# Moving two dummy matmuls from behind a weight piece to in front of it, and one cast from GpSimd to VectorE, in the start of an attention plus MoE kernel

## The chip, the cores and the metric

One core of a Trainium2 chip. The metric is the device time of one execution in microseconds (us), the median of several.

## The reference

```python
def _attn_ref(x, state):                # x [8, 8, 512, 64], state [8, 8, 32, 64]
    scores = scale * np.matmul(x, state.transpose(0, 1, 3, 2))
    a = softmax(scores)                 # (written out in the original)
    xread = np.matmul(a, state)
    scores2 = scale * np.matmul(state, x.transpose(0, 1, 3, 2))
    a2 = softmax(scores2)
    sread = np.matmul(a2, x)
    return np.concatenate([xread, sread], axis=2)

def _moe_ref(x, w_in, w_out):           # 4352 tokens, 512 -> 2048 -> 512
    h = x @ w_in
    g = h * (1.0 / (1.0 + np.exp(-h)))
    return g @ w_out
```

The kernel never forms `xread`. For each batch it multiplies the states by `w_in` (this product is called W1) and applies the normalized scores `a` to W1, which gives the hidden layer at once. So before the first output matmul, batch 0 needs its scores, their transposes, and at least the first columns of W1.

## The kernel before

The loads at the start, in the order of the GpSimd queue. In the trace before the pieces land in this order too, the first at about 8.2 us and the columns 512 to 1023 at 15.5:

```python
    load_w_in(0, 128)        # first W1 piece
    load_w_in(128, 384)      # second W1 piece
    load_w_out(0, 2)         # output weights, blocks 0 and 1
    load_w_out(2, 2)
    nc.gpsimd.dma_start(st1_n..., state[1]...)
    load_w_in(512)           # columns 512 to 1023
    load_w_out(4, 4)
    # ... cut; the rest is issued later
```

The second half of batch 0's input is cast in four quarters, by ScalarE (two), GpSimd and VectorE:

```python
    cast_x(0, nc.scalar, 2, 2, 4, 4)
    cast_x(0, nc.gpsimd, 0, 1, 4, 4)
    pe_transpose_x(0, 0, 2, new_o, (nc.vector, nc.vector))
    cast_x(0, nc.vector, 1, 1, 4, 4)
```

`keep_busy(n, ...)` issues n matmuls on zeros, 128x512 each, whose results nobody reads: dummies, meant to keep TensorE warm while it waits (in the trace before, the first seven, from cold, come 0.43 us apart, later ones 0.216). The stage of the change:

```python
    norm(0, 0)                                    # product on GpSimd
    scores(0, 1, 2); exps(0, 1)                   # (two lines)
    norm(0, 1, ((nc.vector, 0, 4),), 2)           # product on VectorE
    w1_cols(0, [(0, 128)], (nc.scalar, nc.scalar))
    # ... cut: more loads issued
    keep_busy(3, psH, "h1")
    pss0 = w1_mms(0, [(128, 384)])                # the second W1 piece
    keep_busy(2, psH, "h1")
    for c in (0, 2):
        # ... cut: four transposes of the GpSimd half, copies
        at_mms(ps_a, 0, 0, c, 2)
    for c in (0, 2):
        # ... cut: four transposes of the VectorE half, copies
        at_mms(ps_a, 0, 1, c, 2)
    w1_out(0, [(128, 128)], both, pss0)
    upto(1)                                       # first hidden block
    # ... cut
    for ft in range(12):                          # batch 0's output matmuls
        # at ft == 2: w1_mms(0, [(512, 512)]), the W1 matmuls of columns 512 to 1023
```

The softmax here doesn't subtract the row's maximum and nothing guards it: scores larger than these inputs give would overflow.

## Time and profile before

| | before |
|---|---|
| median of 3 runs | 213.05 us (212.82 to 213.13) |
| span of the trace | 211.5 us |
| TensorE busy | 203.7 us, 96% |
| second W1 piece starts | 10.29 us, its weights just landed |
| transposes of the normalized scores start | 11.02 us |
| W1 matmuls of columns 512 to 1023 start | 15.59 us, their weights just landed |

The view of transfers lists an issue with its size and the time from issue to landing. Here are the second W1 piece (384 KB, issued at about 2.4 us) and the columns 512 to 1023 (512 KB, issued at 5.13 us):

```profile
w_in_sb<-in_moe_w_in_dram POOLq DMA_DIRECT2D x1, 384.0 KB, 7.8
w_in_sb<-in_moe_w_in_dram POOLq DMA_DIRECT2D x1, 512.0 KB, 10.4
```

They land at about 10.2 and 15.5 us, exactly where TensorE takes them up.

### The profile page before, as it was taken

The numbers are of one execution on the slowest core, as the hardware profiler recorded it, in microseconds if no ns is written. First come the engines' busy times: TensorE is split into PE (matmuls) and PEld (weight loads), VectorE is DVE, ScalarE is ACT, GpSimd is POOL, SyncE is SP. The second block draws the span as 40 slices with busy tenths as digits, with TensorE's granted clock in tenths as the row PEclk, the third lists the DMA queues.
The fourth block names the chain that finished last, engine by engine and source line by source line (L and its number), as shares of the span: only waits on it lengthen the run. The fifth ranks groups of instructions, "written<-read, shape, count | busy, mean of one in ns | idle before, by whom it ended". The sixth has DMA issues, their size and how long they took to land.

```text
span 211.5 us, 3841 instructions
## 1 busy us (share of the span) xinstructions
PE 203.7 (96%) x1550; PEld 96.8 (46%) x1575; DVE 74.1 (35%) x146; ACT 139.3 (66%) x244; POOL 40.1 (19%) x62
## 2 busy tenths in 40 slices
PE   7799999999999999999999999999999999999993
PEld 2444454444444444444444444444444444466653
DVE  3842257657841236113410653043412306100011
ACT  3866677899577867697569855996775166644410
POOL 8672215503320042012201202000200000000000
PEclk9999999999999999999999999999999999999999
DMA  6999999995549756555935429114221111011112
GB/s 196 193 203 207 287 258 340 226 272 179 103 104 239 205 130 138 122 176 102 233 80 183 104 64 207 50 53 99 80 69 37 63 64 53 0 50 50 53 50 99
DMA packets 42929, 28.65 MB, mean 135 GB/s; under 512 B 28064, under 2 KB 37792, under 8 KB 42912
## 3 DMA queue, kind: packets, MB, share of 16 engines
q1 hardware_dynamic: 36720, 20.65, 37.4%
q0 software_dynamic: 5904, 7.64, 17.4%
q8 instruction: 12, 0.20, 0.4%
q10 hardware_dynamic: 288, 0.13, 0.2%
q14 instruction: 5, 0.04, 0.1%
HBM read 17.43 MB, written 8.91 MB: 125 GB/s over the span
## 4 chain that ended last, share of the span: by engine, by line
PE 90%; DMA 5%; POOL 2%; issue 1%; DVE 0%; POOLq 0%
PE o L566 50%; PE h L525 25%; DMA w_in_sb<-in_moe_w_in_dram 5%; PE ps_w L469 4%; PE h L546 3%; PE o_a L566 3%; PE o_part L588 2%; PE ps_sr L416 1%; PE ps_scT L332 1%; POOL w_in_sb L150 1%; POOL w_out_sb L153 1%; PE ps_sc L306 0%; PE ps_xt L253 0%; DVE W L159 0%; POOL st_n L191 0%
## 5 line engine op out<-in xcount | busy, mean ns | idle before, releaser
L566 PE MATMUL o<-w_out_sb,g 128*128 128x512 bf16 x480 | 129.5, 379 | 1.3 <-issue 0.5
L557 ACT ACTIVATE g<-h 128x512 bf16<-128x512 f32 (+1 forms) x143 | 81.3, 573 | 34.1 <-PE h L525 19.9
L566 PEld LDWEIGHTS <-g 128*128 128x128 bf16 x528 | 50.3, 98 | 59.1 <-issue 3.8
L525 PE MATMUL h<-aT,W 128*128 128x512 bf16 x247 | 73.1, 379 | 0.1
L159 DVE COPY o_sb<-o 128x512 f32<-128x512 f32 x15 | 10.4, 691 | 89.1 <-PE o L566 86.2
L525 PEld LDWEIGHTS <-W 128*128 128x128 bf16 x254 | 24.5, 98 | 30.3 <-issue 0.7
L159 DVE CAST W<-ps_w 128x512 bf16<-128x512 f32 (+2 forms) x36 | 22.2, 658 | 23.2 <-PE ps_w L469 23.2
L157 ACT ACTIVATE W<-ps_w 128x512 bf16<-128x512 f32 (+1 forms) x32 | 16.2, 562 | 11.1 <-PE ps_w L469 11.1
L159 POOL CAST x_nat<-x_f 128x512 bf16<-128x512 f32 x24 | 14.7, 655 | 35.7 <-DMA x_f<-in_x_dram 35.7
L157 ACT ACTIVATE o_sb<-o 128x512 f32<-128x512 f32 x16 | 9.5, 597 | 14.4 <-PE o L566 11.9
L362 POOL TENSOR_TENSOR an<-e,rcn 128x512 bf16<-128x512 bf16 x5 | 7.6, 1517 | 48.0 <-DVE rcn L360 48.0
L469 PE MATMUL ps_w<-w_in_sb,stT 64*32 64x512 bf16 (+2 forms) x264 | 10.3, 373 | 0.6 <-DMA w_in_sb<-in_moe_w_in_dram 0.6
L566 PE MATMUL o_a<-w_out_sb,g 128*128 128x512 bf16 x31 | 9.8, 379 | 0.2
L546 PE MATMUL h<-xmT,w_in_sb 128*128 128x256 bf16 x64 | 9.6, 273 | 0.1
L546 PEld LDWEIGHTS <-w_in_sb 128*128 128x128 bf16 x64 | 6.3, 98 | 3.9
L359 DVE TENSOR_REDUCE rs<-e 128x32 f32<-128x1024 bf16 x5 | 6.1, 1213 | 3.1 <-DMA e<-eT 3.1
L165 PE MATMUL ps_busy<-busy 128*128 128x512 bf16 x15 | 5.9, 497 | 1.2 <-DVE warm L172 1.2
L346 ACT ACTIVATE eT<-ps_scT 128x512 bf16<-128x512 f32 x10 | 5.4, 597 | 1.6 <-PE ps_scT L332 1.6
L786 ACT ACT_TABLE_LOAD x5 | 6.4, 1283 | 0.1
L469 PEld LDWEIGHTS <-stT 64*32 64x32 bf16 x264 | 3.2, 90 | 6.0 <-issue 4.1
L382 POOL TENSOR_TENSOR an<-exp_nat,rc 128x512 bf16<-128x512 bf16 x3 | 3.1, 1048 | 14.8 <-DVE rc L380 14.8
L768 ACT ACT_TABLE_LOAD x4 | 5.1, 1283 | 0.1
(76 smaller groups left out, 99.7 us busy)
## 6 DMA issues: line engine op xcount, KB each, us to landing
out_dram<-o_sb SPq DMA_DIRECT2D x33, 256.0 KB, 2.5
x_f<-in_x_dram SPq DMA_DIRECT2D x4, 1024.0 KB, 6.1
x_f<-in_x_dram POOLq DMA_DIRECT2D x2, 1024.0 KB, 11.9
w_in_sb<-in_moe_w_in_dram POOLq DMA_DIRECT2D x3, 512.0 KB, 10.5
x_f<-in_x_dram SPq DMA_DIRECT2D x2, 512.0 KB, 4.7
w_out_sb<-in_moe_w_out_dram POOLq DMA_DIRECT2D x4, 256.0 KB, 12.0
w_out_sb<-in_moe_w_out_dram POOLq DMA_DIRECT2D x2, 512.0 KB, 12.2
x_f<-in_x_dram POOLq DMA_DIRECT2D x2, 512.0 KB, 15.2
```

Of the source, the lines that this page charges most:

```text
L157: nc.scalar.activation(dst, src, func=COPY, bias=0.0)
L159: eng.tensor_copy(dst, src)
L165: nc.tensor.matmul(ps[:], busy[:, 0:128], busy[:], start=True, stop=True, skip_group_check=True)
L346: nc.scalar.activation(t[:, hg], scT_ps[hg][:], func=EXP, bias=0.0, scale=SCALE)
L359: nc.vector.tensor_reduce(rs[:], e2[b][:], axis=AX, op=ADD)
L362: eng.tensor_tensor(a[:, hg], e2[b][:, hg], rc[:, hg].to_broadcast([128, 4, 4, NS]), op=MULT)
L469: nc.tensor.matmul(pss[f, hg][ds(32 * s, 32), 0:n], stT[ds(r, 64), b, h // 2, s % 2, :], w_in_sb[ds(r, 64), h // 2, ds(f, n)], start=True, ...
L525: nc.tensor.matmul(h_ps[k][:], W1[b][:, hg, ds(128 * ft, 128)], aT[b][:, hg, :, :], start=(hg == 0), stop=(hg == 1), skip_group_check=True,)
L546: nc.tensor.matmul(ps[:, 0:256], w_in_sb[:, kt, ds(128 * ft, 128)], xmT[:, :, kt].rearrange("p t n b -> p t (n b)"), start=(kt == 0), stop ...
L557: nc.scalar.activation(g[:, 0:n], ps[:, 0:n], func=SILU, bias=0.0)
L566: nc.tensor.matmul(outs[tt][:], gt[b * NFT + ft][:, ds(128 * tt, 128)], w_out_sb[:, ft, :], start=(ft == 0), stop=(ft == NFT - 1), skip_gr ...
L786: nc.scalar.activation(warm[:], busy[:, 0:1], func=SILU, bias=0.0)
```

## The change

Its intent: GpSimd and VectorE should not cast side by side, and the dummies should fill the wait in front of the second W1 piece instead of standing between it and the transposes.

```diff
     cast_x(0, nc.scalar, 2, 2, 4, 4)
-    cast_x(0, nc.gpsimd, 0, 1, 4, 4)
     pe_transpose_x(0, 0, 2, new_o, (nc.vector, nc.vector))
-    cast_x(0, nc.vector, 1, 1, 4, 4)
+    cast_x(0, nc.vector, 0, 2, 4, 4)
 ...
-    keep_busy(3, psH, "h1")
+    keep_busy(5, psH, "h1")
     banks[:] = ["a2", "a3"]
     turn[0] = 0
     pss0 = w1_mms(0, [(128, 384)])
-    keep_busy(2, psH, "h1")
```

## The prediction

> **What bounds the kernel now.** I read the views in this order: the page's busy shares, the chain that ended last in order of time, the timelines of the first 16 us by engine, the waits, and the landing times of the weights.
>
> The busy shares say who owns the whole span:
>
> ```profile
> PE 203.7 (96%) x1550; PEld 96.8 (46%) x1575; DVE 74.1 (35%) x146; ACT 139.3 (66%) x244; POOL 40.1 (19%) x62
> ```
>
> TensorE is busy for 203.7 of 211.5 us, so only 7.8 us are idle. The 40-slice row shows TensorE's digits below 9 only in the first two slices (7 and 7, to 10.6 us) and the last. The change lies between 6.6 and 11.7 us, in the start where something is to be had. But what matters is what holds TensorE after it, and there the chain speaks:
>
> ```profile
> 5.13 10.42 DMA w_in_sb<-in_moe_w_in_dram
> 15.55 0.04 issue
> 15.59 0.62 PE ps_w L469 x16
> 16.22 0.32 PE o L566
> ```
>
> Read from the bottom: the matmuls that build W1 from the columns 512 to 1023 of the input weight start at 15.59, 0.04 us after the transfer of these columns landed at 15.55. That transfer was issued at 5.13 and took 10.42 us. Before it the chain lists only GpSimd issuing transfers, back to the first microsecond. Nothing that TensorE, VectorE or GpSimd compute between 5.13 and 15.55 is on it. From 15.59 on the chain is TensorE almost without a break. So the end is set by "weights landed at 15.55" plus TensorE's work from there.
>
> Is TensorE waiting there, or does it only happen to arrive? Its timeline and that of its weight loads:
>
> ```profile
> 14.74 0.81 PE L566 MATMUL o_a<-w_out_sb,g 128*128 128x512 bf16 x3
> 15.47 0.26 PEld L469 LDWEIGHTS <-stT 64*32 64x32 bf16 x16 [0.42 <-issue]
> 15.59 0.62 PE L469 MATMUL ps_w<-w_in_sb,stT 64*32 64x512 bf16 x16
> ```
>
> At the next two such places (21.43 and 26.62) weight load and first matmul start within 0.01 us of one another. Here the matmul starts 0.12 us after its weight load. I read these 0.12 us as a short wait for the landing: TensorE would have been ready at about 15.47. It has no slack against this transfer, it already waits a little.
>
> The stage of the change itself:
>
> ```profile
> 6.61 0.47 POOL L159 CAST x_rows<-x_f 128x256 bf16<-128x256 f32 x1
> 6.65 0.58 DVE L159 CAST x_rows<-x_f 128x256 bf16<-128x256 f32 x1
> ...
> 7.13 0.67 PE L253 MATMUL ps_xt<-ident,x_rows 128*128 128x128 bf16 x8
> ...
> 8.89 0.82 PE L165 MATMUL ps_busy<-busy 128*128 128x512 bf16 x2
> 9.08 1.05 POOL L382 TENSOR_TENSOR an<-exp_nat,rc 128x512 bf16<-128x512 bf16 x1 [2.00 <-DVE rc L380]
> ...
> 9.98 0.70 DVE L382 TENSOR_TENSOR an<-exp_nat,rc 128x512 bf16<-128x512 bf16 x1
> ...
> 10.29 0.36 PE L469 MATMUL ps_w<-w_in_sb,stT 64*32 64x384 bf16 x8 [0.57 <-DMA w_in_sb<-in_moe_w_in_dram]
> ...
> 10.57 0.60 PE L165 MATMUL ps_busy<-busy 128*128 128x512 bf16 x2
> ...
> 11.02 0.61 PE L398 MATMUL ps_at<-ident,an 128*128 128x128 bf16 x8
> 11.33 0.71 DVE L159 COPY aT<-ps_at 128x256 bf16<-128x256 bf16 x3 [0.66 <-PE ps_at L398]
> ```
>
> Three dummies (one record is missing: the program has 3) fill part of the wait for the second W1 piece, whose weights land at about 10.28. Two more stand behind it, and the transposes of the normalized scores start only at 11.02, though GpSimd's half of their input was done at 10.13 and VectorE's at 10.68.
>
> **What the Trainium skill says.** (1) "SBUF — State Buffer", section "Who interferes with whom": VectorE in a two-port mode, which a cast can enter, and GpSimd share a pair of SBUF ports as an exclusive lock, and the one that comes second blocks for the whole instruction. The trace agrees: beside GpSimd's cast of 6.61, VectorE's 256 columns took 0.58 us, while 512 columns without GpSimd took 0.43 us at 5.06. (2) "DMA: Bandwidth & Descriptors", section "Issuing engines are not separate DMA queues": all transfers end on the same 16 engines. The trace agrees: the rate stays at 197 to 206 GB/s from 5 to 20 us, so a transfer queued early lands late. (3) "TensorE: Matmul & The Clock Gate", section "What's actually happening": the array runs at half clock after an idle window of about 3.4 us. The trace agrees as far as it goes: the first seven dummies, from cold, come 0.43 us apart, later matmuls of that size 0.216. The longest idle time of TensorE in the stage is 0.57 us.
>
> **The change part by part.**
> *Casts.* Removed: one GpSimd cast (0.47 us) and one VectorE cast (0.58 us), which ran side by side from 6.61 to 7.23. Added: one VectorE cast of 512 columns, 0.43 us by the twin at 5.06. VectorE is free at about 6.65 to 6.73, so it ends at 7.08 to 7.16 in place of 7.23: 0.07 to 0.15 us earlier. TensorE cannot start these transposes before 7.13 anyway (a dummy began at 6.92 and the next slot is 0.21 later). Their first half waits inside for the second VectorE cast; so VectorE's copy out (7.62) comes some 0.06 us earlier, and scores, exponentials, sums and the two products with it: 10.07 for 10.13 on GpSimd, 10.62 for 10.68 on VectorE.
> *Dummies.* Five stay five. Before the second W1 piece there are now 5 x 0.216 = 1.08 us from about 8.85: the next matmul could start at about 9.93, still before 10.28. So the piece still starts at 10.29, held by its transfer, which nothing here touches (issued before 4 us). Behind it the two dummies go: the transposes move from 11.02 to 10.57, the slot that the first dummy had, a gain of 2 x 0.216 = 0.43 us. Their input: GpSimd's half is there at 10.07; VectorE's half, needed 4 transposes later at about 10.79, is there at 10.62. ScalarE is held by a table load and its warm-up to 11.05 and copies its quarter then instead of at 11.44. So the chain behind (copies, first hidden block, first output matmuls) runs 0.40 to 0.45 us earlier up to the gate.
> *The gate.* At 15.59 TensorE would then be ready at about 15.05, but the weights land at 15.55: its transfer was issued at 5.13, before the first instruction that the change touches. The 0.43 us turn into a wait of some 0.5 us in front of these matmuls. Sum on the path that sets the end: 0.00 to 0.10 us, the remainder for copies that are out of the way earlier.
>
> **The rivals.**
> (a) *The gain passes through.* If, in runs without profiling, the transfer lands some tenths earlier, TensorE and not the transfer is last at 15.5, and up to 0.43 us come through: 212.6. For it: the profiled run took 213.31 us, 0.26 over the median, and part of that may be in transfers. The later gates would allow it: the page gives a median of 10.5 us for the three large input-weight pieces, and 14.1 for the slowest of all; the second was issued at 10.07, so it lands at about 20.6 for a need at 21.43, and the third at 11.61 + 14.1 = 25.7 for 26.62. Against it: the 0.12 us wait in the trace. I give it a quarter, and mostly in part.
> (b) *The dummies become the wait.* If the second piece's weights land before 9.9, five dummies hold it up. But the transposes need VectorE's product at 10.62, and the piece takes 0.28 us, so this costs nothing: 213.0.
> (c) *VectorE becomes the bound,* having taken over GpSimd's cast. Against: without the shared ports its one cast is shorter than its half was. If the cast did take 0.6 us or more, the start would slip 0.1 us and vanish at the same gate: 213.0 to 213.1.
> (d) *TensorE cools* in the new wait at 15.1. Against: 0.5 us is far below the idle window named above; at half clock even 3 us of work would cost 1.5 us, which I hold for very unlikely.
>
> **Range and chances.** 213.05 less 0.05 for the main case, less about 0.1 as a weighted share of rival (a), gives 212.9. Downward the whole of (a) and a little scatter: 212.5. Upward nothing but scatter of the three runs before (212.82 to 213.13) and a little more: 213.2. Two per cent are 4.3 us, ten times all that is at stake: same 0.985, faster 0.01, slower 0.005.
>
> **What would show it.** In the trace after: no GpSimd cast near 6.6 and one VectorE cast of 512 columns of about 0.43 us; the second W1 piece still at 10.2 to 10.4 behind a transfer wait, now shorter than 0.57; the transposes at 10.5 to 10.7; the first output matmul at about 12.3 in place of 12.74; and at 15.5 to 15.6 the W1 matmuls as before, with a TensorE wait of about 0.5 us for the weights. If these matmuls start at 15.2 or before, rival (a) was right and the time should be near 212.6. It is wrong beyond the range if a later stage falls into another order, or the weights' landing moves by more than some tenths.

## The result, and the profile after

The changed kernel took 213.19 us (213.05 to 213.34, 6 runs), the kernel before 213.04 us (212.82 to 213.37, 6 runs) in the same rounds. The ratio is 1.0006, with a 95% interval of 0.9993 to 1.0019: the same. The trace after has a span of 211.4 us, before 211.5.

The timeline after. The columns are start, duration, engine, line, operation, and in brackets the idle time ahead of it with what ended it; the changed source is two lines shorter, so the lines L468 and L397 here are L469 and L398 of before. PE is TensorE's matmuls, PEld its weight loads, DVE VectorE, POOL GpSimd:

```profile
6.88 0.42 DVE L159 CAST x_rows<-x_f 128x512 bf16<-128x512 f32 x1
...
7.37 0.61 PE L253 MATMUL ps_xt<-ident,x_rows 128*128 128x128 bf16 x8
...
9.07 1.25 PE L165 MATMUL ps_busy<-busy 128*128 128x512 bf16 x5
9.25 1.05 POOL L381 TENSOR_TENSOR an<-exp_nat,rc 128x512 bf16<-128x512 bf16 x1 [2.49 <-DVE rc L379]
...
10.15 0.69 DVE L381 TENSOR_TENSOR an<-exp_nat,rc 128x512 bf16<-128x512 bf16 x1
...
10.25 0.36 PE L468 MATMUL ps_w<-w_in_sb,stT 64*32 64x384 bf16 x8
...
10.54 0.76 PE L397 MATMUL ps_at<-ident,an 128*128 128x128 bf16 x8
```

The change did what it was meant to do: the single cast takes 0.42 us, the five dummies stand together, and the transposes start at 10.54 in place of 11.02, although the inputs of this execution came 0.23 us later than in the trace before (first VectorE cast at 5.29, before at 5.06). And here it ends, first in the timeline, then in the chain that ended last (the profile follows it back from the last instruction to what released each one):

```profile
14.41 0.81 PE L565 MATMUL o_a<-w_out_sb,g 128*128 128x512 bf16 x3
15.15 0.09 PEld L468 LDWEIGHTS <-stT 64*32 64x32 bf16 x1 [0.42 <-issue]
15.47 0.62 PE L468 MATMUL ps_w<-w_in_sb,stT 64*32 64x512 bf16 x16 [0.25 <-DMA w_in_sb<-in_moe_w_in_dram]
```

```profile
5.14 10.29 DMA w_in_sb<-in_moe_w_in_dram
15.43 0.04 issue
15.47 0.62 PE ps_w L468 x16
```

TensorE began to load the first state block for these matmuls at 15.15; then it stood idle for 0.25 us, until the columns had landed at 15.43. Before, it started 0.04 us after a landing at 15.55. So the start moved by 0.12 us, exactly as much as the landing moved, and the 0.33 us by which the matmuls ahead came earlier (last output matmuls from 14.41, before from 14.74) became a wait. In this pair of traces the gain is lost at this gate; this is read from two executions, which lie apart in their inputs too.

### The profile page after: what moved, and what is told of

The parts are those of the page before. It is cut to its first block, busy times and chain, and to the rows that moved or that the text cites. A ratio compares the mean times of both kernels' runs of the same rounds, so it can differ in the third digit from the quotient of the medians.

```text
span 211.4 us, 3865 instructions
## 1 busy us (share of the span) xinstructions
PE 205.4 (97%) x1575; PEld 96.7 (46%) x1575; DVE 73.7 (35%) x146; ACT 139.2 (66%) x244; POOL 39.1 (19%) x61
## 4 chain that ended last, share of the span: by engine, by line
PE 91%; DMA 5%; POOL 2%; DVE 0%; issue 0%; POOLq 0%
PE o L565 51%; PE h L524 26%; DMA w_in_sb<-in_moe_w_in_dram 5%; PE ps_w L468 4%; PE h L545 3%; PE o_a L565 3%; PE o_part L587 2%; PE ps_sr L415 1%; PE ps_scT L331 1%; POOL w_in_sb L150 1%; POOL w_out_sb L153 1%; PE ps_sc L305 0%; PE ps_xt L253 0%; DVE W L159 0%; POOL st_n L191 0%; PE ps_at L397 0%
## 5 line engine op out<-in xcount | busy, mean ns | idle before, releaser
L565 PE MATMUL o<-w_out_sb,g 128*128 128x512 bf16 x496 | 132.0, 379 | 0.0
L524 PE MATMUL h<-aT,W 128*128 128x512 bf16 x254 | 74.6, 379 | 0.1
L159 DVE COPY o_sb<-o 128x512 f32<-128x512 f32 x15 | 10.4, 691 | 89.5 <-PE o L565 86.5
L159 POOL CAST x_nat<-x_f 128x512 bf16<-128x512 f32 x24 | 14.1, 630 | 35.0 <-DMA x_f<-in_x_dram 35.0
L468 PE MATMUL ps_w<-w_in_sb,stT 64*32 64x512 bf16 (+2 forms) x264 | 10.3, 373 | 0.3 <-DMA w_in_sb<-in_moe_w_in_dram 0.3
L468 PEld LDWEIGHTS <-stT 64*32 64x32 bf16 x264 | 3.2, 90 | 5.6 <-issue 4.3
```

Source lines behind the costliest of these rows:

```text
L159: eng.tensor_copy(dst, src)
L468: nc.tensor.matmul(pss[f, hg][ds(32 * s, 32), 0:n], stT[ds(r, 64), b, h // 2, s % 2, :], w_in_sb[ds(r, 64), h // 2, ds(f, n)], start=True, ...
L524: nc.tensor.matmul(h_ps[k][:], W1[b][:, hg, ds(128 * ft, 128)], aT[b][:, hg, :, :], start=(hg == 0), stop=(hg == 1), skip_group_check=True,)
L565: nc.tensor.matmul(outs[tt][:], gt[b * NFT + ft][:, ds(128 * tt, 128)], w_out_sb[:, ft, :], start=(ft == 0), stop=(ft == NFT - 1), skip_gr ...
```

## The experiments

The first theory was this gate: TensorE's gain is eaten by the landing of columns 512 to 1023. Four runs were meant to test it, on one chip and with one set of runs of the kernel before (median 212.89 us, 11 runs, 212.73 to 213.63).

**Take the gate away from the changed kernel.** The columns are loaded ahead of the output weights for blocks 2 and 3:

```diff
     load_w_out(0, 2)
-    load_w_out(2, 2)
     nc.gpsimd.dma_start(st1_n..., state[1]...)
     load_w_in(512)
+    load_w_out(2, 2)
     load_w_out(4, 4)
```

> The changed kernel, and in the list of loads the piece of output weights for blocks 2 and 3 stands behind the input weights 512 to 1023 and no longer in front of them, so these land some 1.2 us earlier (about 14.2 in place of 15.43). Gate theory: the W1 matmuls of these columns start when TensorE is ready, at 15.1 to 15.2 in place of 15.47, without a wait for the transfer; the span falls by about 0.3 us and the time to about 0.3 us below the changed kernel, some 0.4 below the kernel before. Rival theory (the 0.4 us of the change are taken by TensorE's own work or by a later wait, not by this transfer): these matmuls start at 15.4 or later, or they start early and the span is the same as before within 0.1 us.

Measured: 212.81 us, ratio to before 0.9993 (0.9978 to 1.0007); the W1 matmuls start at 15.15 without a wait, as the gate theory said. But the 0.4 us below the kernel before that were expected did not come: it is 0.08, inside the noise. And the start without a wait proves less than it seems: the repeat further below, with the old order of loads, does not wait either.

**The same new order in the kernel before.** The same edit, nothing else.

> The kernel before with the same new order of loads, nothing else. Gate theory: TensorE was ready only 0.12 us before the weights landed, so the W1 matmuls start at about 15.45 in place of 15.59 and the time falls by about 0.1 us; it stays 0.3 us above the changed kernel with the new order. Rival theory (the order of loads alone is worth as much as the change, or nothing): the two kernels with the new order are equal within 0.1 us.

Measured: 212.89 us, ratio 0.9996 (0.9983 to 1.0010), and the W1 matmuls start at 15.03. That is not 15.45, and it is even earlier than in the changed kernel. The gate theory had said that without the gate the changed kernel is 0.3 us ahead; it is not. The trace of this run shows why:

```profile
8.95 0.82 PE L165 MATMUL ps_busy<-busy 128*128 128x512 bf16 x3
9.70 0.35 PE L469 MATMUL ps_w<-w_in_sb,stT 64*32 64x384 bf16 x8
9.99 0.61 PE L165 MATMUL ps_busy<-busy 128*128 128x512 bf16 x2
10.43 0.75 PE L398 MATMUL ps_at<-ident,an 128*128 128x128 bf16 x8
```

The second W1 piece starts right behind its three dummies, at 9.70, without a wait: its weights, whose load the new order does not touch, landed 7.0 us after their issue and not 7.8. There was nothing for the dummies to fill.

**More dummies behind the piece.** Two kernels probe the slack from the other side, each with six dummies between the piece and the transposes:

```diff
 # in the changed kernel (five dummies in front)
     pss0 = w1_mms(0, [(128, 384)])
+    keep_busy(6, psH, "h1")
 # in the kernel before (three dummies in front)
-    keep_busy(2, psH, "h1")
+    keep_busy(6, psH, "h1")
```

> The changed kernel with six dummy matmuls (6 x 0.216 = 1.30 us) behind the second W1 piece, in front of the transposes. Gate theory: TensorE had been ready at about 15.15 and the weights landed at 15.43, so the first 0.32 us are free: W1 matmuls start at about 16.45, no wait for the transfer, time up by 0.9 to 1.05 us over the changed kernel. If there were no gate, the time would go up by the full 1.30; if TensorE had far more slack (dummies in the shade of other work), by less than 0.5.

> The kernel before with four more dummies behind the second W1 piece (six there in all, 0.86 us more). Gate theory: 0.12 us free, so W1 matmuls start at about 16.3 to 16.4 and the time rises by about 0.75 us over the kernel before. The time should be that of the changed kernel with six dummies within 0.1 us, for only the casts (0.06 us) and the dummies in front, which lie in a wait for a transfer, are left between them. If the dummies in front cost time of their own, the changed kernel with six is slower by up to 0.4.

Measured: 213.86 and 213.50 us, ratios 1.0044 (1.0031 to 1.0058) and 1.0027 (1.0014 to 1.0041). The expectation that the two are equal within 0.1 us failed; the last sentence of the second one came true instead. The W1 matmuls start at 16.12 and 15.95, earlier than the 16.45 and 16.3 to 16.4 expected, which were counted from the late landings of the first traces. From the first of the front dummies to the W1 matmuls of columns 512 to 1023 the traces count 7.24 us in the first (8.88 to 16.12) and 6.81 in the second (9.14 to 15.95): 0.43, two dummies of 0.216. So with the second piece's weights early (7.1 and 7.0 us here) dummies in front cost what dummies behind cost.

**A second theory** came out of this. The transfers have an early and a late state. The move of two dummies is worth the part of the wait in front of the piece that they fill, at most 0.43 us. When the weights land before the three dummies are through, five dummies and one piece stand ahead of the transposes in either order, and the move is worth nothing. Two plain repeats test it; for the late state, the second piece's load is exchanged with the one behind it, which makes it late on purpose:

```diff
     load_w_in(0, 128)
-    load_w_in(128, 384)
     load_w_out(0, 2)
+    load_w_in(128, 384)
     load_w_out(2, 2)
```

> The kernel before, unchanged, for a second trace. In the four experiments the weights of the second W1 piece landed at about 9.4 in place of 10.2 us. New theory (two states of the transfers): the change is worth min(0.43, landing minus the end of the three dummies) at the transposes, and when the weights land early it is worth nothing there, for five dummies and one piece stand ahead of the transposes in either order. So: with an early landing the piece starts at about 9.6 to 9.7 behind three dummies without a wait, the transposes at 10.35 to 10.45, and the W1 matmuls of the columns 512 to 1023 at 15.0 to 15.1. With a late landing: 10.25, 11.0 and 15.5 to 15.6, as in the first trace. Theory of the gate alone: transposes at 11.0 in any case.

> The changed kernel, unchanged, for a second trace beside that of the kernel before. Two-state theory, early landing: piece at about 10.05 behind five dummies, transposes at 10.35 to 10.45, W1 matmuls of the columns 512 to 1023 at 15.0 to 15.1, all within 0.1 us of the kernel before when both are counted from the start of the first transposes; time equal within 0.1 us. Theory of the gate alone: transposes 0.43 us ahead of those of the kernel before, and TensorE waits for the weights in front of the W1 matmuls.

> The kernel before with the loads of the second W1 piece and of the first two output blocks exchanged, so the weights of the second W1 piece land some 0.6 to 1.3 us later (10.2 to 11.4 by the state) while the columns 512 to 1023 land as before. Two-state theory: second piece at its landing L, transposes at L + 0.72, first output matmuls late by the same, W1 matmuls of columns 512 to 1023 at L + 5.3 (behind their own landing, so no gate there), time up by 0.4 to 1.1 us.

> The changed kernel with the same two loads exchanged. Two-state theory: here the dummies in front fill the whole wait, transposes at L + 0.29, so everything from there to the end is 0.43 us earlier than in the kernel before with the exchange, and the time is 0.35 to 0.45 us less than that kernel's. If the placing of the dummies were worth nothing in any state, the two would be equal within 0.1 us.

The two repeats: 212.91 us (212.77 to 213.37) for the kernel before, 212.94 us (212.69 to 213.32) for the changed one. The landing times and TensorE's timeline of the kernel before, repeated:

```profile
w_in_sb<-in_moe_w_in_dram POOLq DMA_DIRECT2D x1, 384.0 KB, 6.9
...
w_in_sb<-in_moe_w_in_dram POOLq DMA_DIRECT2D x1, 512.0 KB, 9.6
```

```profile
8.96 0.82 PE L165 MATMUL ps_busy<-busy 128*128 128x512 bf16 x3
9.71 0.36 PE L469 MATMUL ps_w<-w_in_sb,stT 64*32 64x384 bf16 x8
10.00 0.60 PE L165 MATMUL ps_busy<-busy 128*128 128x512 bf16 x2
10.44 0.75 PE L398 MATMUL ps_at<-ident,an 128*128 128x128 bf16 x8
...
15.04 0.66 PE L469 MATMUL ps_w<-w_in_sb,stT 64*32 64x512 bf16 x16
```

And of the changed kernel, repeated:

```profile
9.00 1.25 PE L165 MATMUL ps_busy<-busy 128*128 128x512 bf16 x5
10.18 0.36 PE L468 MATMUL ps_w<-w_in_sb,stT 64*32 64x384 bf16 x8
10.47 0.76 PE L397 MATMUL ps_at<-ident,an 128*128 128x128 bf16 x8
...
15.09 0.66 PE L468 MATMUL ps_w<-w_in_sb,stT 64*32 64x512 bf16 x16
```

The piece starts 0.47 us later in the changed kernel, the transposes only 0.03 later, and the changed kernel's row was 0.04 behind from its first line on. Neither kernel waits for columns 512 to 1023: they landed at 5.15 + 9.6 = 14.75 us, and TensorE came at 15.04 and 15.09. Here there is no gate, and no gain that it could take.

The late load: 213.56 us (213.41 to 213.57, 5 runs) for the kernel before, 213.17 us (212.89 to 214.49, 6 runs) for the changed one, a difference of 0.39 as expected, but with a wide scatter: the ratios to before, 1.0029 (1.0017 to 1.0041) and 1.0014 (0.9998 to 1.0030), are not clear of one another. The only trace of the latter fell on its slowest execution (214.49 us): the inputs came late, and TensorE ran a block of eight transposes at 8.45 us in 1.06 us, which takes 0.61 when warm. It could not be laid beside the other, so it was run again, together with each part of the change alone:

> The changed kernel with the two loads exchanged, once more: the first trace of it fell on an execution with late inputs and a TensorE that stayed at half rate until 8.5 us, so it can't be laid beside the other. Two-state theory: second W1 piece at its landing (about 10.4), transposes 0.29 us later (10.7 to 10.8), W1 matmuls of the columns 512 to 1023 at 15.25 to 15.35, against 10.46, 11.20 and 15.65 of the kernel before with the exchange; median time about 213.1.

> The kernel before with the two loads exchanged and the dummies alone moved, the casts as before. If the dummies are all of the gain: transposes 0.29 us behind the piece, as in the changed kernel with the exchange, and a median of about 213.1, within 0.1 us of it. If the casts are part of it: later by what they are worth (0.06 by the prediction, up to 0.4 if they were the cause).

> The kernel before with the two loads exchanged and the casts alone changed, three dummies in front and two behind as before. If the dummies are all of the gain: transposes 0.72 us behind the piece, W1 matmuls of columns 512 to 1023 at about 15.65, median about 213.55. If the casts were the cause: about 213.1. In the trace VectorE's one cast of 512 columns should take about 0.43 us.

The edits of the last two are the late load above plus, of the change, only the dummies or only the casts. The medians were 213.38 us (213.12 to 214.44, 6 runs) for the changed kernel, 213.14 us (212.95 to 213.79, 6 runs) for the dummies alone, 213.58 us (213.39 to 213.64, 5 runs) for the casts alone. The 213.1 expected of the first was missed by 0.3. The ratios to before are 1.0030 (1.0011 to 1.0050), 1.0015 (1.0001 to 1.0029) and 1.0032 (1.0019 to 1.0045): again not clear of one another. The traces have this:

| late load | landing | piece | transposes | W1 matmuls, columns 512 on | piece to these |
|---|---|---|---|---|---|
| before | 10.42 | 10.46 | 11.20 | 15.65 | 5.19 |
| casts alone | 10.37 | 10.41 | 11.14 | 15.60 | 5.19 |
| dummies alone | 10.63 | 10.67 | 10.96 | 15.43 | 4.76 |
| whole change (again) | 10.55 | 10.59 | 10.88 | 15.35 | 4.76 |

The last column is the difference of the two before it that start with "piece" and "W1". It falls by 0.43 us, two dummies, with the dummies moved, and by nothing with the casts. The piece with the wait in front of it, and the W1 matmuls of columns 512 on, in the traces of before (first) and of the whole change (second):

```profile
10.46 0.36 PE L469 MATMUL ps_w<-w_in_sb,stT 64*32 64x384 bf16 x8 [0.70 <-DMA w_in_sb<-in_moe_w_in_dram]
...
15.65 0.66 PE L469 MATMUL ps_w<-w_in_sb,stT 64*32 64x512 bf16 x16
```

```profile
10.59 0.36 PE L468 MATMUL ps_w<-w_in_sb,stT 64*32 64x384 bf16 x8 [0.21 <-DMA w_in_sb<-in_moe_w_in_dram]
...
15.35 0.66 PE L468 MATMUL ps_w<-w_in_sb,stT 64*32 64x512 bf16 x16
```

The wait shrank from 0.70 to 0.21 us: two dummies (0.43), a landing 0.13 later and first dummies 0.18 later (9.12, before 8.94). So the move is worth what it fills of this wait, here all of its 0.43 us. In time, the twelve runs of the whole change with the late load have a median of 213.29 (the middle of 213.25 and 213.32), 0.27 us under the five of the kernel before with it. Taken together after the fact, 12 of the 18 runs with the dummies moved are faster than the fastest of the ten without (213.39); but some are far slower (up to 214.49), and by the ratios alone nothing would be shown.

**What holds the transposes when the weights land early?** The last run leaves three dummies in all, in front, with the new order of loads:

```diff
-    keep_busy(5, psH, "h1")
+    keep_busy(3, psH, "h1")
```

> The changed kernel with the new order of loads (columns 512 to 1023 in front of the output weights for blocks 2 and 3) and only three dummies, all in front of the second W1 piece. It asks what holds the transposes when the weights land early. Theory: VectorE's product, done about 1.7 us after the scores of the second half start and needed by the last four transposes; then the first four start about 0.25 us earlier (at the end of GpSimd's product), the last four and everything behind them do not, and the time is that of the changed kernel with the new order within 0.1 us. Rival: TensorE's own row of work (dummies, piece, transposes) holds them; then two dummies less give 0.3 to 0.43 us, and this kernel beats both.

Measured: 212.91 us (212.81 to 213.41), the kernel before 212.86 in the same rounds, ratio 1.0009 (0.9995 to 1.0023). TensorE's timeline now shows its waits openly:

```profile
9.74 0.35 PE L468 MATMUL ps_w<-w_in_sb,stT 64*32 64x384 bf16 x8
10.31 0.40 PE L397 MATMUL ps_at<-ident,an 128*128 128x128 bf16 x4 [0.21 <-POOL an L381]
10.86 0.40 PE L397 MATMUL ps_at<-ident,an 128*128 128x128 bf16 x4 [0.15 <-DVE an L381]
```

The first four transposes wait for GpSimd's product, the last four for VectorE's. The W1 matmuls of columns 512 on start at 15.11, where the changed kernel with the same order had 15.15. Two dummies less gave nothing: without them VectorE's product sets this stage. It is not far behind: in the repeats the chain that ended last runs through the five dummies, the piece and the transposes, in this run through the product. No version beats the kernel before outside the noise.

## Why the prediction was right or wrong

The time fell into the range (213.19, range 212.5 to 213.2, close to its upper end), and "the same" was right. Both were safe, and the first was partly luck: the centre of 212.9 was 0.15 under the kernel before, and the measured time lies 0.15 over it, within the noise. Which of those executions had the late transfers is known of the two profiled ones alone. Step by step:

- **What bounds the kernel.** Right for the traces at hand: the chain before and after goes through the landing of columns 512 to 1023. It was taken for a fixture of the kernel, and it is not: in the repeats these columns landed at 14.75 and TensorE came later.
- **Casts.** The one cast took 0.42 us as said. The 0.06 us that it was to be worth are in the first pair of traces (eight transposes in 0.61 us, before in 0.67), but not in the repeats (0.61 in both). With the late load nothing of it reaches the end: the casts alone leave the way from piece to W1 matmuls at 5.19 us. With early weights they were not tried alone. The 0.58 us of VectorE's old cast was one draw: in the six traces with the old casts it took 0.28 to 0.64 us. In five of them it ended 0.15 to 0.16 us after GpSimd's cast, whenever it had begun (6.64 to 6.95), which fits the lock that the prediction cites; in the sixth it ended at 6.91, ahead of GpSimd's.
- **Dummies.** The 0.43 us were right where the weights land late. Five dummies were said to take 1.08 us; from the first of them to the piece it is 1.18 (9.07 to 10.25), so in the trace after the piece came directly behind them and not behind its transfer, whose landing at about 10.1 (2.4 + 7.7) was just over. The wait in front of the piece that was to remain was not there.
- **The chain behind.** "0.40 to 0.45 us earlier" was too much; it was 0.33. The last four transposes were said to find VectorE's product ready at 10.62; it was there at 10.84 (10.15 + 0.69), and they waited (the eight took 0.76 us, before 0.61). The inputs' lateness of 0.23 us in this execution, which was not foreseen, explains the product (10.62 + 0.23 = 10.85).
- **The gate.** Right for these two traces, with a smaller wait: 0.25 us in place of 0.5, because TensorE came later (15.15, said 15.05) and the columns landed earlier (15.43, before 15.55).
- **Rival (a)** was thought through wrongly. It let columns 512 to 1023 land earlier and kept the late landing of the second piece. But in the six traces with both loads in their place the two transfers are early or late together: 6.9 to 7.1 and 9.6 to 9.9 us in four, 7.7 to 7.8 and 10.3 to 10.4 in two. When the gate opens, the wait that the dummies were to fill is gone too. So the gain does not pass through; it does not arise. That is the step that put the centre at 212.9 in place of 213.0.
- **Rival (b)** said that early weights make five dummies in front a hold-up that costs nothing, because of VectorE's product. The repeats show that it costs nothing, but first of all for a reason that it did not name: the kernel before has the same five dummies and the same piece ahead of its transposes. The last run shows that the product would hold them too. The two kernels with six dummies behind add that the two in front do cost their 0.43 us as soon as TensorE, and not that product, is last.
- **Rivals (c) and (d)** did not happen; TensorE stayed warm in the wait at 15.15 (the W1 matmuls behind it took 0.62 us, as before). The sum in (d) is short, though: 3 us of full-rate work at half clock would cost 3 us, not 1.5. TensorE's warm-up does matter elsewhere. "TensorE: Matmul & The Clock Gate", section "What's actually happening", says that the ramp depends on a free-running window and differs from run to run; these traces agree (two dummies took 0.61 us at 4.49 in the trace before, 1.03 at 4.64 in its repeat), and the execution of 214.49 us, with its eight transposes of 1.06 us in place of 0.61, fits this.

What stays open: why the transfers were late in the first two traces (7.8 and 7.7 us from issue to landing of the second piece) and early in the seven later ones that left this load in its place (6.9 to 7.1, on three chips). The cause was not looked for. The lateness is there from the first weight piece on (128 KB: 6.7 and 6.6 us against 5.3 to 6.0 in the twelve later traces), and the record does not say on which chip the first two ran, so a difference between chips is as open as one between executions. The other slow executions of the changed kernel with the late load (up to 214.44 us) have no trace. That the kernel before was 0.15 to 0.26 us faster in the later rounds (212.78 to 212.89, first 213.04) would fit earlier landings, but this is argued, not shown.

## What to carry to other kernels

A filler moved into a wait is worth only as much of that wait as exists in the execution at hand: take a second trace before trusting a wait for a transfer, because transfers of one queue can come early or late together, as in the six traces here, and then both the wait and the gate that would swallow its gain vanish at once. Before moving work off the path, list what else the next instruction needs; here it was VectorE's product, less than 0.1 us behind (done at 10.78 in the repeat of the changed kernel, where the transposes start at 10.47 and the last four need it). When a difference lies under the scatter of times, measure distances between two instructions in the traces: here a distance of 5.19 against 4.76 us, the same in two traces each, settled what medians did not.

## What the Trainium skill lacked or had wrong

- "DMA: Bandwidth & Descriptors", section "Bandwidth", gives one duration for each size and nothing on the spread between executions: the same 512 KB piece, issued at the same place of the same queue, landed 10.4 and 10.3 us after its issue in two traces and 9.6 to 9.9 in four others. For a load that TensorE awaits, these 0.4 to 0.8 us were as much as the whole change was worth at best (0.43).
- No page gives the time that a change from whole-array matmuls to packed ones costs; "TensorEngine Tiling (Array Packing)", section "Key Properties", says only that changing the tiling mode drains TensorE. In these traces five dummies of 0.216 us (1.08) were followed by the packed W1 piece 1.18 us after their first start, three of them (0.65) after 0.75: about 0.10 us more, where two dummies in front of whole-array transposes took 0.44 (0.43). That the change of mode is the cause was not tested.
- Nothing that these runs measured was found wrong in the pages used.
